# Replacing a per-channel convolution on transposed input by banded matmuls on untransposed input

## The chip, the cores and the metric

The kernel runs on one core of a Trainium2 chip. The metric is the device time of one execution in microseconds (us). A profile comes from one profiled execution; its span is the time between its first and its last instruction, and the execution's own time is a little longer.

## What is computed

Input `x` is 8 sequences of 4096 rows with 192 channels. Stage one is a causal convolution over the rows with 7 taps; the 192 channels are 8 heads of 24 channels, and the 7 weights of a head (a softmax of 7 numbers) are shared by its channels. Stage two is a two-layer map with 2048 hidden units and the activation h·cos(h).

```python
w = softmax(weight)                       # 8 heads x 7 taps
x_pad = concat([zeros(B, 6, D), x])       # 6 rows of zeros ahead of each sequence
out = einsum('hk,bskhg->bshg', w, x_unf)  # x_unf[b, s, k] = x_pad[b, s + k]
h = out @ w_in                            # 32768 x 192 @ 192 x 2048
return (h * cos(h)) @ w_out               # @ 2048 x 192
```

## The kernel before

The 32768 rows are cut into 64 tiles of 512 rows, 8 to a sequence. All matmuls are bf16 and sum in fp32. The body is written as a loop over the tiles, but the order in which instructions stand on each engine is fixed when the program is built: a scheduler mixes the steps of neighbouring tiles on each engine, and each engine then goes through its own list in order, waiting on semaphores where a step needs another engine's result. The buffers come from pools that rotate: `x_bf`, `xT`, `xT_o`, `conv_sb` and `g_sb` two each, `x_f32`, `cos_sb` and `o_sb` three; of the PSUM tiles `h_ps` three, and `ps_t`, `conv_ps` and `o_ps` one each.

For each tile:

- `prep_tile` (L115 to L138): SyncE's queue loads 512 rows into `x_f32` (L118, 384 KB), GpSimd casts them to bf16 in four pieces (`x_bf`, L121), TensorE turns them in 8 transposes (`ps_t`, L126) so that channels lie on the partitions (two halves of 96), and ScalarE copies the two halves out of PSUM (`xT`, L127 and L128). GpSimd puts the last 6 columns of the tile before in front (L133), or zeros at the start of a sequence (L131), and makes a copy of `xT` shifted by one column (`xT_o`, L136), which the odd taps read.
- `conv_tile` (L140 to L152): for each of 7 taps and 2 channel halves one matmul with 512 moving columns (L148), 14 in all, whose weights are a 96x96 diagonal matrix of that tap's weights (`diagW`, L100, made once at the start). They sum in `conv_ps`, and VectorE copies the two halves to `conv_sb` (L150, L151), which is again channels by rows.
- Hidden layer (L161 to L168): for each of 16 blocks of 128 hidden units two matmuls with 512 columns (L164) fill one `h_ps`, ScalarE takes the cosine of it (L167), and VectorE multiplies `h_ps` by the cosine into `g_sb` (L168). An `h_ps` comes free when both have read it.
- Output layer (L174 to L183): for each of 4 pieces of 128 rows 16 matmuls with 192 columns (L180) sum in half of an `o_ps`, and VectorE copies that half out (L182). The second half's matmuls wait for the copy of the first half. The tile's output leaves with one transfer (L183).

In the loop the preparation and convolution of tile it+1 stand between the hidden layer and the output layer of tile it. At the start of the program a chain of small steps on VectorE and ScalarE makes the softmax and `wtab`, from which `diagW` is made, while the two weight matrices are loaded and cast.

## Time and profile before

| what | value |
| --- | --- |
| median of 4 runs | 1119.2 us (1118.15 to 1119.48) |
| the profiled execution's own time | 1119.48 us |
| its span | 1117.7 us |
| TensorE busy (matmuls / weight loads) | 1066.2 us / 684.8 us |
| VectorE, ScalarE, GpSimd busy | 814.4, 699.2, 154.3 us |
| matmuls and weight loads | 7554 of each |
| transfer of a tile's input, issue to landing | 3.4 us |

A row of a group gives the line, the engine, the operation, the tiles that it writes and reads, their shapes, the count, the busy time in us and the mean duration in ns, and then how long the engine was idle just before, and who released it. PEld is the weight load of TensorE, which has records of its own. Matmuls follow each other faster than their durations say, since each includes the way through the array; so the spacing of a run of matmuls is worked out from the run's length less one duration. A row of the timeline gives the start, the length of a run of like instructions, and what they are. The chain of waits is the work that ended last, followed back from the end.

### The profile page before, as it was taken

How to read it: one execution, taken by the hardware profiler on the slowest of the kernel's cores; microseconds unless marked ns; L12 is line 12 of the kernel's file. 1: busy time of each engine (PE TensorE's matmuls, PEld its weight loads, DVE VectorE, ACT ScalarE, POOL GpSimd, SP SyncE). 2: the span in 40 equal slices, each digit the busy share in tenths (PEclk: the TensorE clock that was granted, in tenths of full speed). 3: DMA queues.
4: the chain of work that ended last, by engine and by line, in shares of the span. 5: the costliest groups of instructions: out<-in, count | busy, mean ns of one | idle time of the engine just before them, and what ended most of it. 6: DMA issues, size and time to landing. Idle time of an engine off the chain costs nothing.

```text
span 1117.7 us, 19647 instructions
## 1 busy us (share of the span) xinstructions
PE 1066.2 (95%) x7554; PEld 684.8 (61%) x7554; DVE 814.4 (73%) x1432; ACT 699.2 (63%) x1159; POOL 154.3 (14%) x392
## 2 busy tenths in 40 slices
PE   3999999999999999999999999999999999999997
PEld 2566666566666665666666666666656666666664
DVE  1877777777777777777777777777777777777775
ACT  4765665666656656656656666566566566665663
POOL 2111111111101101111111111011011111111100
PEclk9999999999999999999999999999999999999999
DMA  7111111111101101111111111011011111110000
GB/s 197 44 49 38 57 45 42 57 43 43 57 30 56 58 29 58 54 33 57 45 42 58 43 44 57 29 57 58 29 57 55 32 58 43 43 57 28 16 30 29
DMA packets 69982, 54.74 MB, mean 49 GB/s; under 512 B 2112, under 2 KB 69696, under 8 KB 69696
## 3 DMA queue, kind: packets, MB, share of 16 engines
q1 hardware_dynamic: 69888, 53.49, 15.9%
q8 instruction: 59, 0.97, 0.4%
q14 instruction: 35, 0.29, 0.1%
HBM read 28.31 MB, written 25.17 MB: 48 GB/s over the span
## 4 chain that ended last, share of the span: by engine, by line
PE 66%; ACT 15%; issue 9%; POOL 6%; DMA 1%; DVE 1%; POOLq 0%; SPq 0%; ACTq 0%
PE o_ps L180 25%; PE h_ps L164 22%; PE conv_ps L148 16%; ACT cos_sb L167 10%; POOL xT_o L136 6%; ACT xT L128 3%; PE ps_t L126 2%; ACT xT L127 2%; DMA x_f<-in_x_dram 1%; POOL x_bf L121 1%; DVE g_sb L168 1%; DVE conv_sb L150 0%; DVE o_sb L182 0%; POOLq L209 0%; POOLq L136 0%
## 5 line engine op out<-in xcount | busy, mean ns | idle before, releaser
L167 ACT ACTIVATE cos_sb<-h_ps,halfpi 128x512 bf16<-128x512 f32 x1024 | 644.2, 692 | 391.1 <-PE h_ps L164 390.3
L168 DVE TENSOR_TENSOR g_sb<-h_ps,cos_sb 128x512 bf16<-128x512 f32 x1024 | 654.6, 686 | 222.9 <-ACT cos_sb L167 222.1
L164 PE MATMUL h_ps<-conv_sb,w_in_sb 96*128 96x512 bf16 x2048 | 561.9, 378 | 18.9 <-DVE g_sb L168 12.4
L180 PE MATMUL o_ps<-w_out_sb,g_sb 128*128 128x192 bf16 x4096 | 433.2, 246 | 2.3 <-DVE o_sb L182 1.3
L180 PEld LDWEIGHTS <-g_sb 128*128 128x128 bf16 x4096 | 349.6, 97 | 114.5 <-issue 24.5
L164 PEld LDWEIGHTS <-w_in_sb 96*128 96x128 bf16 x2048 | 195.1, 97 | 181.0 <-issue 39.1
L121 POOL CAST x_bf<-x_f 128x192 bf16<-128x192 f32 x256 | 78.4, 346 | 759.1 <-PE ps_t L126 734.3
L148 PEld LDWEIGHTS <-diagW 96*96 96x96 bf16 x896 | 110.5, 123 | 107.7 <-issue 19.4
L148 PE MATMUL conv_ps<-xT,diagW 96*96 96x512 bf16 x512 | 164.9, 382 | 1.0 <-ACT xT L127 1.0
L148 PE MATMUL conv_ps<-xT_o,diagW 96*96 96x512 bf16 x384 | 116.2, 382 | 9.0 <-POOL xT_o L136 8.4
L182 DVE COPY o_sb<-o_ps 128x192 f32<-128x192 f32 x256 | 89.6, 350 | 10.7 <-PE o_ps L180 5.8
L136 POOL COPY xT_o<-xT 96x1034 bf16<-96x1034 bf16 x64 | 67.2, 1050 | 174.5 <-ACT xT L128 174.5
L150 DVE CAST conv_sb<-conv_ps 96x512 bf16<-96x512 f32 x64 | 43.9, 686 | 55.6 <-PE conv_ps L148 55.6
L126 PE MATMUL ps_t<-ident,x_bf 128*96 128x128 bf16 x512 | 51.2, 222 | 10.7 <-POOL x_bf L121 10.7
L126 PEld LDWEIGHTS <-x_bf 128*96 128x96 bf16 x512 | 40.1, 125 | 19.9 <-POOL x_bf L121 10.8
L151 DVE CAST conv_sb<-conv_ps 96x512 bf16<-96x512 f32 x64 | 43.3, 677 | 0.0
L127 ACT COPY xT<-ps_t 96x512 bf16<-96x512 bf16 x64 | 37.2, 581 | 7.0 <-PE ps_t L126 7.0
L128 ACT COPY xT<-ps_t 96x512 bf16<-96x512 bf16 x64 | 37.8, 591 | 0.0
L133 POOL COPY xT<-xT 96x12 bf16<-96x12 bf16 x56 | 10.7, 191 | 0.0
L100 DVE TENSOR_SCALAR diagW<-ident,wtab 96x96 bf16<-96x96 bf16 x14 | 2.2, 238 | 6.8 <-ACT wtab L79 6.8
L76 PE MATMUL wtab_ps<-wsm,sel 8*96 8x7 bf16 x2 | 0.3, 225 | 5.5 <-DVE sel L73 5.5
L94 ACT CAST w_out_sb<-w_out_f 128x3072 bf16<-128x3072 f32 x1 | 2.8, 2752 | 2.7 <-DMA w_out_f<-in_moe_w_out_dram 2.7
(26 smaller groups left out, 11.2 us busy)
## 6 DMA issues: line engine op xcount, KB each, us to landing
x_f<-in_x_dram SPq DMA_DIRECT2D x64, 384.0 KB, 3.4
out_dram<-o_sb SPq DMA_DIRECT2D x64, 384.0 KB, 2.6
w_in_f<-in_moe_w_in_dram SPq DMA_DIRECT2D x2, 768.0 KB, 7.2
w_out_f<-in_moe_w_out_dram SPq DMA_DIRECT2D x1, 1536.0 KB, 12.8
w_sb<-in_weight_dram SPq DMA_DIRECT2D x1, 0.2 KB
```

The lines of the kernel that those rows point to most:

```text
L121: nc.gpsimd.tensor_copy(out=x_bf[:, s, :], in_=x_f32[:, s, :])
L126: nc.tensor.transpose(ps_t[:, c, s, :], x_bf[:, s, c * HD : (c + 1) * HD], ident)
L127: nc.scalar.copy(xT[:, 0, PAD:], ps_t[:, 0, :, :])
L128: nc.scalar.copy(xT[:, 1, PAD:], ps_t[:, 1, :, :])
L136: nc.gpsimd.tensor_copy(out=xT_o[:, :, 0 : T + PAD - 1], in_=xT[:, :, 1 : T + PAD])
L148: nc.tensor.matmul(out=conv_ps[:, c, :], lhsT=diagW[:, c * K + k, :], rhs=rhs_src, start=(k == 0), stop=(k == K - 1))
L150: nc.vector.tensor_copy(out=conv_sb[:, 0, :], in_=conv_ps[:, 0, :])
L164: nc.tensor.matmul(out=h_ps, lhsT=w_in_sb[:, c, f * 128 : (f + 1) * 128], rhs=conv_sb[:, c, :], start=(c == 0), stop=(c == 1))
L167: nc.scalar.activation(out=cos_sb, in_=h_ps, func=AF.Sin, bias=halfpi, scale=1.0)
L168: nc.vector.tensor_tensor(out=g_sb[:, f, :], in0=h_ps, in1=cos_sb, op=ALU.mult)
L180: nc.tensor.matmul(out=o_ps[:, s2, 0:D], lhsT=g_sb[:, f, s * 128 : (s + 1) * 128], rhs=w_out_sb[:, f, :], start=(f == 0), stop=(f == NF - 1))
L182: nc.vector.tensor_copy(out=o_sb[:, s, :], in_=o_ps[:, s2, 0:D])
```

## The change

The convolution is no longer done on the transposed input with one diagonal matrix per tap. It is done on the input as it was loaded, rows on the partitions: the weights of a matmul are now a 128x128 banded matrix, one for each head (`band`), which holds the 7 taps on 7 diagonals, and the moving operand is the 24 channels of that head. A second matrix (`bandhi`) adds what reaches over from the next 128 rows. So each 128 rows take 8 heads x 2 matmuls with 24 columns, and a tile 64 of them in place of 14 with 512 columns. Their result (`ct_ps`, a PSUM tile for two pieces of 128 rows, two of them) is copied to `ct_sb`, by VectorE for the first piece and by ScalarE for the second. Only then come the 8 transposes, and ScalarE and VectorE copy a half each to `convT`, which the hidden layer reads where it read `conv_sb`.

The input is loaded 6 rows earlier, so that row r of a block holds the first tap of output row r. The last block of a tile needs 6 more rows: they come by a small transfer of their own (`hx`, 6x192) and go through a buffer that GpSimd has set to zero (L157 to L160). At the start of a sequence VectorE clears 6 rows of `x_f32` and the load is split in two. Removed are `xT`, the shifted copy `xT_o` (L136), the copying of the last 6 columns (L133) and `diagW`. The preparation of tile it+2 now follows the convolution of tile it+1; before, the preparation of it+1 stood ahead of it.

At the start of the program 8 copies on ScalarE spread the softmax weights, one matmul hands them to all 128 partitions (`wb`), and VectorE builds `band` with 8 multiplications and 48 multiply-adds of 128x128 and `bandhi` with 11 small products and sums.

```diff
+    for ci in range(K - 1):
+        wv = wb3[:, :, 6 - ci : 7 - ci].to_broadcast([128, H, PAD])
+        mv = mc[:, ci : ci + 1, :].to_broadcast([128, H, PAD])
+        nc.vector.tensor_tensor(out=bh if ci == 0 else htmp, in0=mv, in1=wv, op=ALU.mult)
+        if ci:
+            nc.vector.tensor_tensor(out=bh, in0=bh, in1=htmp, op=ALU.add)
+    for h in range(H):
+        b = band[:, h, :]
+        nc.vector.tensor_scalar(out=b, in0=identx[:, 0:128], scalar1=wb[:, h * K : h * K + 1], scalar2=None, op0=ALU.mult)
+        for k in range(1, K):
+            nc.vector.scalar_tensor_tensor(out=b, in0=identx[:, k : k + 128], scalar=wb[:, h * K + k : h * K + k + 1],
+                                           in1=b, op0=ALU.mult, op1=ALU.add)
...
     def prep_tile(it):
...
-        nc.sync.dma_start(out=x_f32, in_=xf[t0 : t0 + T, :].rearrange("(n p) d -> p n d", p=128))
+        if it % TPB == 0:
+            nc.vector.memset(x_f32[0:PAD, 0, :], 0.0)
+            nc.sync.dma_start(out=x_f32[PAD:128, 0, :], in_=xf[t0 : t0 + 128 - PAD, :])
+            nc.sync.dma_start(out=x_f32[:, 1:4, :],
+                              in_=xf[t0 + 128 - PAD : t0 + T - PAD, :].rearrange("(n p) d -> p n d", p=128))
+        else:
+            nc.sync.dma_start(out=x_f32, in_=xf[t0 - PAD : t0 + T - PAD, :].rearrange("(n p) d -> p n d", p=128))
...
-        xT = xT_pool.tile([HD, 2, T + PAD], BF16)
-        ps_t = xtp.tile([HD, 2, 4, 128], BF16)
-        for c in range(2):
-            for s in range(4):
-                nc.tensor.transpose(ps_t[:, c, s, :], x_bf[:, s, c * HD : (c + 1) * HD], ident)
-        nc.scalar.copy(xT[:, 0, PAD:], ps_t[:, 0, :, :])
-        nc.scalar.copy(xT[:, 1, PAD:], ps_t[:, 1, :, :])
...
-        nc.gpsimd.tensor_copy(out=xT_o[:, :, 0 : T + PAD - 1], in_=xT[:, :, 1 : T + PAD])
+        hx = hx_pool.tile([128, 2, D], FP32)
+        nc.sync.dma_start(out=hx[0 : PAD, 0, :], in_=xf[t0 + T - PAD : t0 + T, :])
+        nc.gpsimd.memset(hx[:, 1, :], 0.0)
+        nc.gpsimd.tensor_copy(out=hx[0:PAD, 1, :], in_=hx[0:PAD, 0, :])
+        hx_bf = hx_pool.tile([128, D], BF16)
+        nc.gpsimd.tensor_copy(out=hx_bf, in_=hx[:, 1, :])
...
     def conv_tile():
-        for k in range(K):
-            for c in range(2):
-                rhs_src = xT[:, c, k : k + T] if k % 2 == 0 else xT_o[:, c, k - 1 : k - 1 + T]
-                nc.tensor.matmul(out=conv_ps[:, c, :], lhsT=diagW[:, c * K + k, :],
-                                 rhs=rhs_src, start=(k == 0), stop=(k == K - 1))
-        nc.vector.tensor_copy(out=conv_sb[:, 0, :], in_=conv_ps[:, 0, :])
-        nc.vector.tensor_copy(out=conv_sb[:, 1, :], in_=conv_ps[:, 1, :])
+        for sp in range(2):
+            ct_ps = ct_ps_pool.tile([128, 2, D], FP32)
+            for s2 in range(2):
+                s = sp * 2 + s2
+                nxt = x_bf[:, s + 1, :] if s < 3 else state["hx_bf"]
+                for h in range(H):
+                    nc.tensor.matmul(out=ct_ps[:, s2, h * G : (h + 1) * G], lhsT=band[:, h, :],
+                                     rhs=x_bf[:, s, h * G : (h + 1) * G], start=True, stop=False)
+                    nc.tensor.matmul(out=ct_ps[:, s2, h * G : (h + 1) * G], lhsT=bandhi[:, h, :],
+                                     rhs=nxt[:, h * G : (h + 1) * G], start=False, stop=True)
+                if s2 == 0:
+                    nc.vector.tensor_copy(out=ct_sb[:, s, :], in_=ct_ps[:, s2, :])
+                else:
+                    nc.scalar.copy(ct_sb[:, s, :], ct_ps[:, s2, :])
         ps_t = xtp.tile([HD, 2, 4, 128], BF16)
         for c in range(2):
             for s in range(4):
-                nc.tensor.transpose(ps_t[:, c, s, :], x_bf[:, s, c * HD : (c + 1) * HD], ident)
+                nc.tensor.transpose(ps_t[:, c, s, :], ct_sb[:, s, c * HD : (c + 1) * HD], ident)
+        nc.scalar.copy(convT[:, 0, :], ps_t[:, 0, :, :])
+        nc.vector.tensor_copy(out=convT[:, 1, :], in_=ps_t[:, 1, :, :])
```

How the order on the engines changes is seen at three places in the middle of the program. The first is TensorE's list in the kernel before, where the convolution of the next tile (`conv_ps`) is reached: `h_ps` belongs to the hidden layer, `o_ps` to the output layer, and the engine named in brackets is the one whose semaphore the row waits for.

```order
L180 MATMUL o_ps<-w_out_sb,g_sb 128x192
L148 LDWEIGHTS diagW
L148 MATMUL conv_ps<-xT_o,diagW 96x512 [waits Pool_49]
L148 LDWEIGHTS diagW
L148 MATMUL conv_ps<-xT_o,diagW 96x512
L164 LDWEIGHTS w_in_sb
L164 MATMUL h_ps<-conv_sb,w_in_sb 128x512 [waits DVE_49]
L164 LDWEIGHTS w_in_sb
L164 MATMUL h_ps<-conv_sb,w_in_sb 128x512
L148 LDWEIGHTS diagW
L148 MATMUL conv_ps<-xT,diagW 96x512
```

The convolution's third and fourth matmul wait there for GpSimd's shifted copy, and all that stands behind them waits with them. In the changed kernel TensorE's list has, at the place where the second 128 rows of a `ct_ps` begin:

```order
L201 MATMUL h_ps<-convT,w_in_sb 128x512 [waits DVE_49]
L201 LDWEIGHTS w_in_sb
L201 MATMUL h_ps<-convT,w_in_sb 128x512
L174 LDWEIGHTS band
L174 MATMUL ct_ps<-x_bf,band 128x24 [waits DVE_49]
L176 LDWEIGHTS bandhi
L176 MATMUL ct_ps<-hx_bf,bandhi 128x24 [waits Pool_49]
L174 LDWEIGHTS band
L174 MATMUL ct_ps<-x_bf,band 128x24
L176 LDWEIGHTS bandhi
L176 MATMUL ct_ps<-hx_bf,bandhi 128x24
```

Each matmul of 24 columns has a weight load of its own ahead of it; the first one waits for VectorE's copy of the first 128 rows out of the same PSUM tile, and the first one that reads `hx_bf` for GpSimd.

The second place is TensorE's list in the changed kernel a little ahead of these rows, where the transposes (`ps_t`) of the finished 128-row pieces stand:

```order
L201 LDWEIGHTS w_in_sb
L201 MATMUL h_ps<-convT,w_in_sb 128x512 [waits DVE_49]
L201 LDWEIGHTS w_in_sb
L201 MATMUL h_ps<-convT,w_in_sb 128x512
L218 LDWEIGHTS g_sb
L218 MATMUL o_ps<-w_out_sb,g_sb 128x192
L185 LDWEIGHTS ct_sb [waits Activation_49]
L185 MATMUL ps_t<-ident,ct_sb 96x128
L201 LDWEIGHTS w_in_sb
L201 MATMUL h_ps<-convT,w_in_sb 128x512 [waits DVE_49]
```

The transposes, which opened the preparation before, now follow the convolution, and matmuls of the output and the hidden layer stand between them.

The third place is ScalarE's list in one tile, before:

```order
L167 ACTIVATE cos_sb<-h_ps,halfpi 128x512 [waits DVE_49,PE_49] x8
L127 COPY xT<-ps_t 96x512 [waits PE_49,Pool_49]
L167 ACTIVATE cos_sb<-h_ps,halfpi 128x512 [waits DVE_49,PE_49] x3
L128 COPY xT<-ps_t 96x512
L167 ACTIVATE cos_sb<-h_ps,halfpi 128x512 [waits DVE_49,PE_49] x4
```

and in the changed kernel:

```order
L204 ACTIVATE cos_sb<-h_ps,halfpi 128x512 [waits DVE_49,PE_49] x13
L181 CAST ct_sb<-ct_ps 128x192 [waits PE_49]
L204 ACTIVATE cos_sb<-h_ps,halfpi 128x512 [waits DVE_49,PE_49] x3
L181 CAST ct_sb<-ct_ps 128x192 [waits DVE_49,PE_49]
L204 ACTIVATE cos_sb<-h_ps,halfpi 128x512 [waits DVE_49,PE_49] x2
L186 COPY convT<-ps_t 96x512 [waits PE_49]
```

Two copies of 512 columns between the cosines have become two of 192 columns and one of 512.

89 lines of the change are left out of this document (49 added, 40 removed).

## The prediction

> **What bounds the kernel now.** I read the page first, for the engines and the chain of waits.
>
> ```profile
> span 1117.7 us, 19647 instructions
> PE 1066.2 (95%) x7554; PEld 684.8 (61%) x7554; DVE 814.4 (73%) x1432; ACT 699.2 (63%) x1159; POOL 154.3 (14%) x392
> PE 66%; ACT 15%; issue 9%; POOL 6%; DMA 1%; DVE 1%; POOLq 0%; SPq 0%; ACTq 0%
> ```
>
> TensorE is busy nearly throughout, but a third of the chain lies elsewhere: ScalarE, GpSimd and "issue". So a matmul saved and a wait saved may both count. Next I read one tile in the timeline, for its period and for the spacing of each kind of matmul.
>
> ```profile
> 504.47 0.37 SPq L183 DMA_DIRECT2D out_dram<-o_sb  x1
> ...
> 511.40 0.59 PE L148 MATMUL conv_ps<-xT_o,diagW 96*96 96x512 bf16 x2
> ...
> 512.70 0.59 PE L148 MATMUL conv_ps<-xT,diagW 96*96 96x512 bf16 x2
> ...
> 513.54 0.55 PE L126 MATMUL ps_t<-ident,x_bf 128*96 128x128 bf16 x7
> ...
> 515.14 1.49 PE L180 MATMUL o_ps<-w_out_sb,g_sb 128*128 128x192 bf16 x16
> ...
> 520.74 1.46 PE L164 MATMUL h_ps<-conv_sb,w_in_sb 96*128 96x512 bf16 x6
> ...
> 521.49 0.37 SPq L183 DMA_DIRECT2D out_dram<-o_sb  x1
> ```
>
> ```profile
> L164 PE MATMUL h_ps<-conv_sb,w_in_sb 96*128 96x512 bf16 x2048 | 561.9, 378 | 18.9 <-DVE g_sb L168 12.4 <-DVE conv_sb L150 1.0
> L180 PE MATMUL o_ps<-w_out_sb,g_sb 128*128 128x192 bf16 x4096 | 433.2, 246 | 2.3 <-DVE o_sb L182 1.3 <-DVE g_sb L168 1.0
> L180 PEld LDWEIGHTS <-g_sb 128*128 128x128 bf16 x4096 | 349.6, 97 | 114.5 <-issue 24.5 <-DVE g_sb L168 2.3
> L126 PE MATMUL ps_t<-ident,x_bf 128*96 128x128 bf16 x512 | 51.2, 222 | 10.7 <-POOL x_bf L121 10.7
> L126 PEld LDWEIGHTS <-x_bf 128*96 128x96 bf16 x512 | 40.1, 125 | 19.9 <-POOL x_bf L121 10.8 <-issue 0.9
> ```
>
> A tile's output leaves every 521.49 - 504.47 = 17.02 us, and 64 tiles make 1089 us of the span. Spacing is a run less one duration, over the steps between: hidden layer (1.46 - 0.378)/5 = 0.2164 us, output layer (1.49 - 0.246)/15 = 0.0829, transposes (0.55 - 0.222)/6 = 0.055. The two convolution rows are six matmuls apart: 1.30/6 = 0.217. Each spacing is shorter than the matmul's own duration, and the transposes' 0.055 is even shorter than their weight load's 0.125: loads run under the matmuls ahead of them. A tile then needs on TensorE 32 x 0.2164 + 64 x 0.0829 + 14 x 0.217 + 8 x 0.055 = 6.92 + 5.31 + 3.04 + 0.44 = 15.71 us, and 17.02 - 15.71 = 1.31 us are waits. The chain in order of time, and the engines' busy time in that stretch, say where.
>
> ```profile
> 506.08 0.39 ACT xT L127
> ...
> 508.28 0.60 ACT xT L128
> ...
> 509.00 1.06 POOL xT_o L136
> ...
> 510.11 0.59 PE conv_ps L148 x2
> ```
>
> ```profile
> 504.33:510.11 5.78, 5.33 (x31) 2.79 (x30) 4.50 (x9) 5.75 (x11) 2.33 (x6) 1.00 0.46 136
> ```
>
> From 504.33 to 510.11 ScalarE is the last (5.75 of 5.78 us busy: nine cosines and the two copies), then GpSimd's shifted copy; TensorE drips one hidden block at a time. From 510.11 on TensorE alone sets the pace. This is the wait that the change addresses.
>
> **Part by part.** *Convolution on TensorE.* Out go 3.04 us a tile. In come 64 pairs of a 128x128 weight load and a matmul of 24 columns; the trace has no such pair, and all hangs on its spacing p. From below: 24 columns at the output layer's rate, 24/192 x 0.0829 = 0.010 us. From above, hidden: the transposes, 128 columns and a load each, go at 0.055, so a pair with fewer columns and the quicker load (97 ns against 125) should not need more. From above, not hidden: the whole 0.097 of a load. The nearest in size are two matmuls of 7 columns at the start.
>
> ```profile
> 5.46 0.31 PE L76 MATMUL wtab_ps<-wsm,sel 8*96 8x7 bf16 x2 [5.46 <-DVE sel L73]
> ...
> 22.87 1.06 PE L148 MATMUL conv_ps<-xT,diagW 96*96 96x512 bf16 x2
> ...
> 23.73 1.06 PE L148 MATMUL conv_ps<-xT_o,diagW 96*96 96x512 bf16 x2
> ...
> L76 PE MATMUL wtab_ps<-wsm,sel 8*96 8x7 bf16 x2 | 0.3, 225 | 5.5 <-DVE sel L73 5.5
> ```
>
> They are 0.31 - 0.225 = 0.085 apart, at a time when the clock is low: the convolution's matmuls there are (23.73 - 22.87)/2 = 0.43 apart, twice the 0.217 of later. Halved, 0.085 is 0.0425, with a 96-column load; I take p = 0.040, so 64 x 0.040 = 2.56 us a tile. Transposes, hidden and output layer stay: 6.92 + 5.31 + 0.44 = 12.67. Sum 15.23, 0.48 less.
>
> *The waits.* The hop over GpSimd (1.06 us) is gone: the banded matmuls read `x_bf`, which GpSimd casts a whole tile early.
>
> ```profile
> L167 ACT ACTIVATE cos_sb<-h_ps,halfpi 128x512 bf16<-128x512 f32 x1024 | 644.2, 692 | 391.1 <-PE h_ps L164 390.3
> L121 POOL CAST x_bf<-x_f 128x192 bf16<-128x192 f32 x256 | 78.4, 346 | 759.1 <-PE ps_t L126 734.3 <-DMA x_f<-in_x_dram 14.4 <-issue 10.4
> L136 POOL COPY xT_o<-xT 96x1034 bf16<-96x1034 bf16 x64 | 67.2, 1050 | 174.5 <-ACT xT L128 174.5
> L127 ACT COPY xT<-ps_t 96x512 bf16<-96x512 bf16 x64 | 37.2, 581 | 7.0 <-PE ps_t L126 7.0
> L150 DVE CAST conv_sb<-conv_ps 96x512 bf16<-96x512 f32 x64 | 43.9, 686 | 55.6 <-PE conv_ps L148 55.6
> L182 DVE COPY o_sb<-o_ps 128x192 f32<-128x192 f32 x256 | 89.6, 350 | 10.7 <-PE o_ps L180 5.8
> 1109.77 0.36 DVE L182 COPY o_sb<-o_ps 128x192 f32<-128x192 f32 x1 [1.57 <-PE o_ps L180]
> 1110.19 1.48 PE L180 MATMUL o_ps<-w_out_sb,g_sb 128*128 128x192 bf16 x16 [0.45 <-DVE o_sb L182]
> x_f<-in_x_dram SPq DMA_DIRECT2D x64, 384.0 KB, 3.4
> ```
>
> What is late next is ScalarE again: 16 cosines of 644.2/1024 = 0.63 us, while only three `h_ps` exist. Its copies cost about the same as before (2 x 0.35 + 0.58 = 1.28 us against 2 x 0.58 = 1.16, a 192-column copy priced by VectorE's), VectorE's too (2 x 0.35 + 0.69 against 2 x 0.69). But TensorE has some fifty pairs that need neither, and the order puts them among the hidden blocks. Bounds of the remaining wait: 0 if they fill everything, 1.31 if nothing is gained; I take the half, 0.65. New waits: the second 128 rows of each `ct_ps` wait for VectorE's copy of the first, the transposes for ScalarE's copy, and everything behind on TensorE waits with them. Uncovered, one costs 0.42 us, as at the end of the program (1109.77 to 1110.19), where nothing stands between. In the order, hidden and output matmuls stand between, so I count them at nothing; that cover gone is a rival. On ScalarE and VectorE the copies that wait hold the cosines and products behind them; they wait for pairs that TensorE has done before it turns to other blocks, so again nothing.
>
> *GpSimd and SyncE.* GpSimd loses 1.05 us a tile and gains a zeroing, a small copy and a cast, by the 0.346 us of its cast at most 1.0 together; it was busy 14%. SyncE gets one 4.6 KB transfer per tile more and, eight times, the input in two; the input is issued over a tile ahead of its use and lands in 3.4 us. If the small transfer waited for its buffer, the output and the next input behind it on SyncE's queue would wait as well; with a tile of slack I count nothing.
>
> *The start.*
>
> ```profile
> 5.06 0.34 DVE L73 TENSOR_TENSOR sel<-ge,le 8x192 bf16<-8x192 f32 x1
> ...
> 12.20 2.25 DVE L100 TENSOR_SCALAR diagW<-ident,wtab 96x96 bf16<-96x96 bf16 x14 [6.79 <-ACT wtab L79]
> ...
> 18.76 1.07 PE L148 MATMUL conv_ps<-xT,diagW 96*96 96x512 bf16 x2 [0.67 <-ACT xT L127]
> ...
> 26.23 1.46 PE L164 MATMUL h_ps<-conv_sb,w_in_sb 96*128 96x512 bf16 x6 [0.67 <-DVE conv_sb L150]
> ```
>
> Before, convolution starts at 18.76 us, after the input has landed, and the first hidden block at 26.23. Now VectorE has 56 steps of 128 columns and some 11 small ones after about 7 us. By the spacing of the 14 multiplications (2.25/14 = 0.16) they end near 18 us, hidden by the input; by the 0.34 of the product at 5.06 they end near 30. At 0.25, 56 x 0.25 + 11 x 0.2 = 16.2, they end at 23.2; the last pairs, two copies, the transposes and two copies more make 4 to 7 us, so the first hidden block stands near 30, 4 later. Bounds 0 and 10.
>
> *Sum.* Per tile 15.23 + 0.65 = 15.88, 1.14 less than 17.02; 64 x 1.14 = 73 us less, 4 more at the start. The profiled execution took 1119.48 us, 0.3 more than the median of 1119.2: 1119.5 - 73 + 4 = 1050 us.
>
> **The rivals.** *A: the weight loads show.* If a load is not hidden by a matmul of 24 columns, each pair takes the 0.097 of its row: 6.21 us a tile, 18.88 with the rest, with 0.3 of waits 19.18; 64 x 2.16 + 4 = 142 more, 1262 us. It decides from p = (17.02 - 0.06 - 0.45 - 12.67)/64 = 0.060 on. Against it: both the output layer and the transposes hide theirs, the latter at 0.055. For it: they have more columns to hide under. The Trainium skill (TensorE: Matmul & The Clock Gate, Back-to-back issue gap) gives about 81 ns per matmul for a stream of load and matmul pairs at 128 columns; the transposes' 0.055 does not agree, and by its figure the change would be estimated as slower, near 1196 us.
>
> *B: pairs are cheaper.* Midway between 0.010 and 0.0425, p = 0.026: 1.66 us a tile, less work to fill the waits, say 1.0: 15.33, 64 x 1.69 - 4 = 104 less, 1015 us. For it: the 7-column pairs had loads of 96 columns, the slower kind (125 against 97 ns). The same section of the Trainium skill has an issue floor of about 25 ns for matmuls of up to 64 columns; no row here shows it yet.
>
> *C: pairs cost as much as transposes,* 0.055: 3.52, with 0.45 of waits 16.64; 64 x 0.38 - 4 = 20 less, 1099 us. For it: each pair is two instructions, and no pair in the trace goes faster at the high clock.
>
> *D: the copies show.* If the two waits for VectorE's copy, the wait for ScalarE's last copy and the two halves of `convT` (0.6 each) stood open in every tile, that is 3 x 0.42 + 1.2 = 2.5 us: 15.23 + 2.5 = 17.7, 64 x 0.7 + 4 = 49 more, 1168 us. It decides from 17.02 - 0.06 - 15.23 = 1.73 us on. Against it: the work that stands between in the order.
>
> **How the numbers follow.** Forecast (p from 0.033 to 0.047) 0.40, B 0.28, C 0.19, A 0.08, D 0.05. B's lower end, p = 0.022 with 1.1 of waits, is 15.18 a tile, 64 x 1.84 - 4 = 114 less, 1006; C with the start 10 late in place of 4 and 0.05 more of waits is 1099 + 6 + 3 = 1108. From 1005 to 1108 the range holds the forecast and most of B and C. A difference of 0.2%, about 2 us, is what a measurement can tell here. Faster: the forecast, B, and C but for 0.02: 0.85; within 0.2%: 0.02; slower: A and D, 0.13.
>
> **What would show it.** Right: a run of ct_ps pairs at 0.033 to 0.047 each, outputs leaving every 15.6 to 16.1 us, GpSimd gone from the chain, the first hidden block near 30 us. Pairs at 0.06 or more mean A; TensorE idle before ct_ps or ps_t behind a VectorE or ScalarE copy, by more than 1.7 us a tile, means D; a hidden layer that waits for ScalarE as long as before means that the half I took off the waits is wrong.

## The result and the profile after

| | before | changed |
| --- | --- | --- |
| median | 1119.21 us (1118.15 to 1120.04, 13 runs) | 992.46 us (991.91 to 992.95, 8 runs) |
| ratio | | 0.8868, 95% interval 0.886 to 0.8877 |
| span of the profiled execution | 1117.7 us | 990.6 us |

The medians and ratios here and below leave out two slow executions, one of e3_before_no_hop (1799.22 us at a granted clock of 0.561) and one of e9_rows64 (1563.5 us at 0.816).

The change takes off 127 us, almost twice the 69 that were forecast, and the time lies below the range. The page of the changed kernel, its engines and its chain of waits by engine and by line:

```profile
span 990.6 us, 26393 instructions
PE 959.8 (97%) x10753; PEld 681.2 (69%) x10753; DVE 811.7 (82%) x1567; ACT 720.7 (73%) x1230; POOL 140.2 (14%) x459
PE 96%; DMA 1%; ACT 1%; DVE 1%; POOL 0%; issue 0%; SPq 0%; POOLq 0%
```

TensorE was 66% of the chain and is now 96%; GpSimd's 6% is gone, and ScalarE's 15% is 1%. So the time is nearly the sum of TensorE's work, and the price of a pair decides. The timeline shows it, in the middle of the run:

```profile
507.05 0.81 PE L201 MATMUL h_ps<-convT,w_in_sb 96*128 96x512 bf16 x3
507.82 1.48 PE L218 MATMUL o_ps<-w_out_sb,g_sb 128*128 128x192 bf16 x16
...
510.22 0.18 PE L174 MATMUL ct_ps<-x_bf,band 128*128 128x24 bf16 x1
510.25 0.17 PE L176 MATMUL ct_ps<-x_bf,bandhi 128*128 128x24 bf16 x1
...
510.65 0.17 PE L176 MATMUL ct_ps<-x_bf,bandhi 128*128 128x24 bf16 x1
```

From 510.22 to 510.65 stand 18 matmuls of pairs (the middle ones are left out here), 0.43/17 = 25 ns apart, though every one has its own load of 128x128 weights, which takes 96 ns by its records on the page. The forecast had 40 ns for the spacing. Hidden and output matmuls keep their spacing. The outputs leave at these times, the third and the fifty-ninth:

```profile
78.94 0.41 SPq L221 DMA_DIRECT2D out_dram<-o_sb  x1
...
913.40 73.91 SPq L221 DMA_DIRECT2D out_dram<-o_sb  x6
```

The outputs' own rows give the first and the last, of the changed kernel and of the one before:

```profile
L221 SPq DMA_DIRECT2D out_dram<-o_sb x64: 372/384/406, 50.5 to 986.9; - x64
```

```profile
L183 SPq DMA_DIRECT2D out_dram<-o_sb x64: 372/372/388, 48.9 to 1114.0; - x64
```

The steady period is (913.40 - 78.94)/56 = 14.90 us, where it was 17.02. TensorE needs 6.92 + 5.31 + 0.44 + 64 x 0.025 = 14.27 of it, and 0.63 are waits. From first to last output it is 936.4 us in place of 1065.1, which is 128.7 less; the first output is 1.6 later. That loss goes with TensorE's pace at the start: two hidden matmuls take 0.59 us at 30 us in the kernel before, and still 1.06 in the changed one, where 0.59 is reached only after 34 us. The rows of the changed kernel and of the one before:

```profile
30.89 1.06 PE L201 MATMUL h_ps<-convT,w_in_sb 96*128 96x512 bf16 x2
```

```profile
29.91 0.59 PE L164 MATMUL h_ps<-conv_sb,w_in_sb 96*128 96x512 bf16 x2
```

What TensorE still waits for, by the table of waits (us in total, times, longest):

```profile
PEld L185 <- ACT ct_sb L181: 23.0, 83, 0.5
PEld L218 <- issue: 18.1, 75, 0.6
PEld L218 <- DVE g_sb L205: 7.8, 25, 0.8
```

PEld is TensorE's weight load. The largest is a new wait, the transposes' for ScalarE's copy of `ct_sb`: 23.0/64 = 0.36 us a tile. The second 128 rows' wait for VectorE's copy is 0.4 us in the whole run.

### The profile page after: what moved, and what is told of

It reads as the page before. It is cut to its first block, busy times and chain, and to the rows that moved or that the text cites. A ratio compares the mean times of both kernels' runs of the same rounds, so it can differ in the third digit from the quotient of the medians.

```text
span 990.6 us, 26393 instructions
## 1 busy us (share of the span) xinstructions
PE 959.8 (97%) x10753; PEld 681.2 (69%) x10753; DVE 811.7 (82%) x1567; ACT 720.7 (73%) x1230; POOL 140.2 (14%) x459
## 4 chain that ended last, share of the span: by engine, by line
PE 96%; DMA 1%; ACT 1%; DVE 1%; POOL 0%; issue 0%; SPq 0%; POOLq 0%
PE h_ps L201 46%; PE o_ps L218 35%; PE ct_ps L176 5%; PE ct_ps L174 5%; PE ps_t L185 4%; DMA x_f<-in_x_dram 1%; ACT convT L186 1%; POOL x_bf L154 0%; ACT cos_sb L204 0%; DVE g_sb L205 0%; DVE o_sb L220 0%; SPq L119 0%; SPq L125 0%; SPq L49 0%; DVE ct_sb L179 0%
## 5 line engine op out<-in xcount | busy, mean ns | idle before, releaser
L201 PE MATMUL h_ps<-convT,w_in_sb 96*128 96x512 bf16 x2048 | 579.1, 380 | 2.4 <-DVE g_sb L205 0.4
L174 PE MATMUL ct_ps<-x_bf,band 128*128 128x24 bf16 x2048 | 148.8, 174 | 15.9 <-DVE band L112 12.3
L174 PEld LDWEIGHTS <-band 128*128 128x128 bf16 x2048 | 131.6, 96 | 45.7 <-DVE band L114 9.5
L176 PEld LDWEIGHTS <-bandhi 128*128 128x128 bf16 x2048 | 125.9, 96 | 45.4 <-issue 13.4
L176 PE MATMUL ct_ps<-x_bf,bandhi 128*128 128x24 bf16 x1536 | 116.0, 173 | 0.2
L185 PEld LDWEIGHTS <-ct_sb 128*96 128x96 bf16 x512 | 53.8, 123 | 42.5 <-ACT ct_sb L181 23.0
L185 PE MATMUL ps_t<-ident,ct_sb 128*96 128x128 bf16 x512 | 81.1, 231 | 0.1
L179 DVE CAST ct_sb<-ct_ps 128x192 bf16<-128x192 f32 x128 | 43.5, 349 | 5.2 <-PE ct_ps L176 5.2
L181 ACT CAST ct_sb<-ct_ps 128x192 bf16<-128x192 f32 x128 | 40.6, 319 | 5.3 <-PE ct_ps L176 5.2
L186 ACT COPY convT<-ps_t 96x512 bf16<-96x512 bf16 x64 | 36.5, 570 | 1.0 <-PE ps_t L185 1.0
L160 POOL CAST hx_bf<-hx 128x192 bf16<-128x192 f32 x64 | 22.0, 344 | 0.1
L157 POOL MEMSET hx<- 128x192 f32 x64 | 16.4, 258 | 3.7
```

Of the source, the lines that this page charges most:

```text
L174: nc.tensor.matmul(out=ct_ps[:, s2, h * G : (h + 1) * G], lhsT=band[:, h, :], rhs=x_bf[:, s, h * G : (h + 1) * G], start=True, stop=False)
L176: nc.tensor.matmul(out=ct_ps[:, s2, h * G : (h + 1) * G], lhsT=bandhi[:, h, :], rhs=nxt[:, h * G : (h + 1) * G], start=False, stop=True)
L179: nc.vector.tensor_copy(out=ct_sb[:, s, :], in_=ct_ps[:, s2, :])
L181: nc.scalar.copy(ct_sb[:, s, :], ct_ps[:, s2, :])
L185: nc.tensor.transpose(ps_t[:, c, s, :], ct_sb[:, s, c * HD : (c + 1) * HD], ident)
L186: nc.scalar.copy(convT[:, 0, :], ps_t[:, 0, :, :])
```

## The experiments

My theory after the two traces: a pair costs 25 ns whatever its columns, which is the whole of the missed gain, and the waits are as forecast. Rivals: the pair costs its load or its columns, and 25 ns is chance; or the gain came from waits. A second question is what made the row wrong from which the prediction took p. All times below are medians; the ratio is to the kernel before, timed on the same chip, with its 95% interval.

| run | time, us | ratio |
| --- | --- | --- |
| e1_halves, 128 pairs of 12 columns | 1082.49 | 0.9682 (0.9665 to 0.9698) |
| e2_wide48, 32 pairs of 48 | 980.55 | 0.8767 (0.8754 to 0.8781) |
| e2b_wide96, 16 pairs of 96 | 964.32 | 0.8623 (0.861 to 0.8636) |
| e6_k6, second matmul on 6 rows | 1570.53 | 1.4045 (1.4024 to 1.4066) |
| e9_rows64, on 64 rows | 1548.84 | 1.3838 (1.3782 to 1.3894) |
| e9b_rows32, on 32 rows | 1548.2 | 1.3849 (1.383 to 1.3868) |
| e12_wtab16 (before, 16 small pairs) | 1119.58 | one execution |
| e14_forms (changed, forms at its end) | 992.8 | one execution |
| e3_before_no_hop, no shifted copy | 1086.56 | 0.9702 (0.9685 to 0.9718) |
| e5_hps4, four `h_ps` | 1053.5 | 0.9406 (0.939 to 0.9422) |
| e7_rowmajor, transposes' loops exchanged | 990.12 | 0.8844 (0.883 to 0.8857) |
| e8_half_bands, half the bands built | 989.44 | 0.8835 (0.8823 to 0.8848) |
| e11_gpsimd_bands, two bands by GpSimd | 991.9 | 0.887 (0.8858 to 0.8882) |
| e13_strided96, 16 pairs, same result | 963.72 | 0.8616 (0.8603 to 0.8629) |
| e15_strided48, 32 pairs, same result | 965.68 | 0.8629 (0.8615 to 0.8644) |
| e16_scalar_copies, e13 with ScalarE's copies | 973.8 | 0.8703 (0.8691 to 0.8715) |

### What a pair costs

**e1_halves: twice as many pairs, half as wide.**

```diff
-                for h in range(H):
-                    nc.tensor.matmul(out=ct_ps[:, s2, h * G : (h + 1) * G], lhsT=band[:, h, :],
-                                     rhs=x_bf[:, s, h * G : (h + 1) * G], start=True, stop=False)
+                for q in range(2 * H):
+                    h, G2 = q // 2, G // 2
+                    nc.tensor.matmul(out=ct_ps[:, s2, q * G2 : (q + 1) * G2], lhsT=band[:, h, :],
+                                     rhs=x_bf[:, s, q * G2 : (q + 1) * G2], start=True, stop=False)
...
```

> Each banded matmul of 24 columns is split into two of 12 with the same weights, so a tile has 128 pairs in place of 64 and computes the same. Theory 1 (a pair costs a fixed 25 ns however few its columns are, with its weight load hidden): the spacing stays at 25 ns, a tile needs 64 x 0.025 = 1.6 us more on TensorE, of which at most the 0.63 us of waits that remain can be filled: 992 + 64 x (1.0 to 1.6) = 1056 to 1095 us. Rival (the 25 ns belong to 24 columns and shrink with them): spacing near 13 ns, 985 to 1000 us.

The timeline, with 30 steps from the first row to the last:

```profile
507.01 0.17 PE L175 MATMUL ct_ps<-x_bf,band 128*128 128x12 bf16 x1
...
507.76 0.17 PE L175 MATMUL ct_ps<-x_bf,band 128*128 128x12 bf16 x1
```

The spacing stays 25 ns, and the time rises by 90 us: 64 more pairs of 25 ns are 1.6 us a tile, 102 us over 64, of which some 0.2 us a tile went into waits that were there. Fewer columns save nothing at this size; each pair costs 25 ns.

**e2_wide48 and e2b_wide96: fewer, wider pairs.** A matmul takes two or four heads' columns with the first head's weights; the other heads' weights are left out. The second matmul is edited alike; with 96 columns the step is 4.

```diff
-                for h in range(H):
-                    nc.tensor.matmul(out=ct_ps[:, s2, h * G : (h + 1) * G], lhsT=band[:, h, :],
-                                     rhs=x_bf[:, s, h * G : (h + 1) * G], start=True, stop=False)
+                for h in range(0, H, 2):
+                    nc.tensor.matmul(out=ct_ps[:, s2, h * G : (h + 2) * G], lhsT=band[:, h, :],
+                                     rhs=x_bf[:, s, h * G : (h + 2) * G], start=True, stop=False)
...
```

> Two heads share one pair of 48 columns, with the weights of the first of the two: 32 pairs a tile, the other head's taps are left out. Theory 1 (fixed 25 ns): spacing 25 ns again, since 48 columns at the output layer's rate (0.0829/192 each) are 21 ns; 0.8 us a tile less, 992 - 51 = 941, to 955 if waits take some of it back. Rival (the cost grows with the columns, or a fixed part plus a column part): spacing 36 to 50 ns, 32 x 0.036 to 0.05 = 1.15 to 1.6 us, 963 to 995 us.

> Four heads share one pair of 96 columns, with the weights of the first of the four: 16 pairs a tile, the other heads' taps are left out. Theory 1 (the larger of 25 ns and the columns' own time): 96 columns at the output layer's rate are 41 ns, so the spacing is 41 to 44 ns, 16 x 0.042 = 0.67 us a tile, 0.93 less: 992 - 59 = 933, to 950 if the waits grow. If a floor were a property of the weight load alone and added to the columns, the spacing would be 25 + 41 = 66 ns, 1.06 us a tile and 958 us or more.

The timeline of the first and of the second:

```profile
507.68 0.18 PE L174 MATMUL ct_ps<-x_bf,band 128*128 128x48 bf16 x1
507.70 0.18 PE L176 MATMUL ct_ps<-x_bf,bandhi 128*128 128x48 bf16 x1
```

```profile
513.34 0.20 PE L174 MATMUL ct_ps<-x_bf,band 128*128 128x96 bf16 x1
513.38 0.20 PE L176 MATMUL ct_ps<-x_bf,bandhi 128*128 128x96 bf16 x1
```

48 columns still go at 25 ns, 96 at 41: the spacing is the larger of 25 ns and the columns' own time (0.43 ns each, as at 192 and 512), and the load lies under it. Both times lie above what theory 1 put and where the rivals had them; it is the spacing that decides for theory 1. Of the 51 us that 32 fewer pairs save, the 48-column run shows only 12, and the 96-column one 28 of some 60. Much of the rest became waits; the table of the first:

```profile
PEld L185 <- ACT ct_sb L181: 51.1, 113, 0.6
PEld L218 <- DVE g_sb L205: 25.0, 64, 0.7
```

The transposes' wait has grown by 28 us and the one for VectorE's products from 7.8 to 25: TensorE is no longer the only bound.

**e6_k6, e9_rows64, e9b_rows32: fewer rows in the second matmul.** Only 6 rows of `bandhi` are not zero. In e6_k6 the second matmul and its load take these 6, and GpSimd's zeroing goes; in the others 64 and 32.

```diff
-                    nc.tensor.matmul(out=ct_ps[:, s2, h * G : (h + 1) * G], lhsT=bandhi[:, h, :],
-                                     rhs=nxt[:, h * G : (h + 1) * G], start=False, stop=True)
+                    nc.tensor.matmul(out=ct_ps[:, s2, h * G : (h + 1) * G], lhsT=bandhi[0:PAD, h, :],
+                                     rhs=nxt[0:PAD, h * G : (h + 1) * G], start=False, stop=True)
...
```

> The second matmul of each pair, for what reaches over from the next 128 rows, uses only the 6 rows of its weights and of its operand that are not zero; the buffer that GpSimd zeroed is then not needed, and GpSimd's zeroing and one of its two small steps are gone. It computes the same. Theory 1 (fixed 25 ns, a load's size hidden; GpSimd far from the bound): same within 0.5%, 988 to 997 us, and spacing still 25 ns. Rival (the rows that a load or a matmul reads set the price): half of the pairs get cheaper, up to 32 x 0.02 = 0.64 us a tile, 951 to 975 us.

It missed by over 570 us, which is why the other two were run:

> The changed kernel, where the second matmul of each pair (and its weight load) takes 64 rows in place of 128; only rows 0 to 5 of its weights are not zero, so the result is the same. With 6 rows the pairs' matmuls went 114 to 119 ns apart and the run took 1570 us. Theory 1 (any change of the row count between neighbours costs it): 110 to 120 ns per matmul again and about 1400 to 1580 us. Rival 1 (it is the small count, in which few of the array's rows are used, that costs it; hidden blocks with 96 rows and output blocks with 128 follow each other in the changed kernel at no cost): 25 ns and 985 to 1000 us.

> As the last one, with 32 rows in place of 64. Theory 1 (any change of the row count): 110 to 120 ns per matmul and about 1400 to 1580 us. Rival 1 (small counts alone): 25 ns and 985 to 1000 us if 32 rows are enough, 110 to 120 ns if they still are too few; with the run of 64 rows this brackets the point.

The timeline with 64 rows, and two windows of the same run (the last three columns: granted clock, share of the DMA engines, GB/s):

```profile
503.12 0.18 PE L176 MATMUL ct_ps<-x_bf,bandhi 64*128 64x24 bf16 x1
...
503.83 0.18 PE L176 MATMUL ct_ps<-x_bf,bandhi 64*128 64x24 bf16 x1
```

```profile
500.00:515.00 15.00, 15.00 (x125) 10.54 (x123) 9.60 (x18) 8.44 (x14) 1.22 (x5) 0.98 0.17 54
516.00:530.00 14.00, 14.00 (x84) 8.66 (x82) 5.12 (x10) 5.06 (x9) 2.08 (x7) 0.50 0.10 30
```

Six steps take 0.71 us, so each step between 128 and 64 rows costs 0.12 us, as with 6 and 32 rows: 64 x (0.117 - 0.025) = 5.9 us a tile, 377 over the run. The other 180 to 200 go with stretches at half the clock (0.50 in the second window); the mean granted clock is 0.835, 0.823 and 0.809 with 64, 32 and 6 rows, where the changed kernel has 1.000. What makes the clock fall is open. Theory 1's numbers hold in both runs, but as worded it goes too far: hidden blocks with 96 rows and output blocks with 128 follow each other at no such price in all these kernels.

**e12_wtab16 and e14_forms: which property of a pair costs.** The first repeats the two small pairs at the start of the kernel before, from which the prediction took its p; the second puts nine runs of 16 matmuls of 24 columns behind the changed kernel's last tile.

```diff
-    for c in range(2):
+    for c in [0, 1] * 8:
         nc.tensor.matmul(out=wtab_ps[:, c * K : (c + 1) * K], lhsT=sel[:, c * HD : (c + 1) * HD], rhs=wsm,
                          start=True, stop=True)
```

> The kernel before, with the two matmuls of 7 columns at its start (8 rows, 96 columns of weights) issued eight times over, 16 in a row with a weight load each; the result is the same. The prediction took its p from the 85 ns between the two, halved for the low clock. Theory 1 (the first step after an idle time is longer, and two matmuls show only that): the first two stand about 85 ns apart or more, all later ones 25 to 30, low clock or not. Rival (85 ns is the steady spacing of such pairs at the low clock): all about 85. A third outcome would be above 85 throughout, if matmuls with few rows are slow even when all have the same count.

```diff
+    def one(r, m):
+        return dict(out=ct_ps[0:m, 0, 0:24], lhsT=ident[0:r, 0:m], rhs=mv[0:r, :], start=True, stop=True)
+    for _ in range(16):
+        nc.tensor.matmul(**one(128, 128))
...
```

> The changed kernel, and behind its last tile nine runs of 16 matmuls of 24 columns, each with its own weight load, whose results nobody reads: 128, 96, 64 and 8 rows with 128 columns of weights; 128 and 8 rows with 96 columns of weights; and 128x128 in turn with 96x128, 64x128 and 128x96. It asks what made the pair before the prediction 85 ns, and what made the 6-, 32- and 64-row pairs 114 to 119. Theory 1 (a load goes ahead under the running matmul only if it takes more than 64 rows, or the matmul does): 25 ns for 128 and 96 rows and for 128 in turn with 96; 75 to 120 ns for 64 and 8 rows, alone or in turn; 96 columns of weights alone cost nothing (25 to 45 ns). Rival 1 (only a change of the row count costs): 64 and 8 rows alone at 25 ns, in turn at 115. Rival 2 (weights of 96 columns are what made the old pair slow): 128x96 at 75 ns or more, 8x128 at 25.

The first run's timeline, and the second's:

```profile
5.48 1.44 PE L76 MATMUL wtab_ps<-wsm,sel 8*96 8x7 bf16 x16 [5.48 <-DVE sel L73]
```

```profile
979.59 0.55 PE L230 MATMUL ct_ps<-g_sb,ident 128*128 128x24 bf16 x16
979.99 0.35 PE L232 MATMUL ct_ps<-g_sb,ident 96*128 96x24 bf16 x8
...
981.80 0.56 PE L234 MATMUL ct_ps<-g_sb,ident 64*128 64x24 bf16 x16
...
983.72 0.56 PE L236 MATMUL ct_ps<-g_sb,ident 8*128 8x24 bf16 x16
984.21 0.53 PE L238 MATMUL ct_ps<-g_sb,ident 128*96 128x24 bf16 x8
...
986.32 0.88 PE L240 MATMUL ct_ps<-g_sb,ident 8*96 8x24 bf16 x16
...
987.55 0.17 PE L245 MATMUL ct_ps<-g_sb,ident 128*128 128x24 bf16 x1
987.66 0.18 PE L246 MATMUL ct_ps<-g_sb,ident 64*128 64x24 bf16 x1
...
989.30 0.18 PE L246 MATMUL ct_ps<-g_sb,ident 64*128 64x24 bf16 x1
```

A run less one duration (0.17 to 0.19 us), over its steps: 128, 96, 64 and 8 rows all go at 25 to 26 ns as long as the count stays the same, and 128 and 96 in turn too; 128 and 64 in turn at (989.30 - 987.55)/15 = 0.117 us. Weights of 96 columns go at 0.34/7 = 49 ns with 128 rows and 0.69/15 = 46 with 8; weights of 128 and 96 columns in turn at 35 on average. So two separate prices: a step between 128 rows and 64 or fewer, and weights of 96 columns. At the start, 16 in a row stand (1.44 - 0.225)/15 = 81 ns apart: the 85 of the prediction was a steady spacing, as the rival had it, not a first step. Of the forms theory 1 falls; rival 1 holds for the rows, and rival 2 for the columns in part (49, not 75). The Trainium skill (TensorE: Matmul & The Clock Gate, Weight-path perf modes) says that the fast weight load is taken only with 128 columns of weights; 25 against 46 to 49 ns agrees. The Trainium skill also says (TensorEngine Tiling (Array Packing), Key Properties) that a change of the tiling mode drains TensorE, and lists 64 rows as a mode of their own (Available Configurations there); 117 in turn and 25 alone agree, though no run shows the mode itself.

### What the waits are worth

**e3_before_no_hop: the kernel before without GpSimd's shifted copy.**

```diff
-        nc.gpsimd.tensor_copy(out=xT_o[:, :, 0 : T + PAD - 1], in_=xT[:, :, 1 : T + PAD])
...
-                rhs_src = xT[:, c, k : k + T] if k % 2 == 0 else xT_o[:, c, k - 1 : k - 1 + T]
+                rhs_src = xT[:, c, k : k + T]
```

> The kernel before, with one edit: the odd taps read xT itself at an odd column, so GpSimd's shifted copy xT_o (1.06 us between ScalarE's second copy and the first convolution matmul) is gone; the 14 matmuls of 512 columns stay. It prices the hop alone. Theory 1 (the hop was half of the 1.31 us of waits that a tile had): 0.5 to 1.0 us a tile less, 32 to 64 us, 1055 to 1087 us, with the spacing of the convolution's matmuls at 0.217 for odd taps too. Rival 1 (hidden blocks fill that stretch anyway, and the waits are ScalarE's): 1105 to 1120 us. Rival 2 (an odd start column makes a matmul slower, as a misaligned read): the six odd matmuls of a tile at 0.3 us or more, and 1140 us or more.

```profile
512.26 1.90 PE L143 MATMUL conv_ps<-xT,diagW 96*96 96x512 bf16 x8
```

Odd and even taps go at (1.90 - 0.38)/7 = 0.217 us, so rival 2 is out. The hop was worth 32.5 us, 0.51 a tile. With the 64 x (3.04 - 1.60) = 92 us that TensorE saves on the convolution this makes 124.6, against 126.8 measured: the two parts of the change add up to within 2 us.

**e5_hps4 and e7_rowmajor: what the last 0.63 us are.** For the fourth `h_ps`, `wb_ps` comes from a pool that is closed once `wb` is copied.

```diff
-    h_ps_pool = ctx.enter_context(tc.tile_pool(name="h_ps", bufs=3, space=bass.MemoryType.PSUM))
+    h_ps_pool = ctx.enter_context(tc.tile_pool(name="h_ps", bufs=4, space=bass.MemoryType.PSUM))
...
```

> The changed kernel with four buffers of h_ps in place of three (the PSUM space comes from the weight broadcast at the start, whose buffer is given back early). It asks what the 0.63 us a tile are in which TensorE still waits. Theory 1 (they are waits for the convolution's own copies, 23.0 us of it the transposes' for ScalarE's copy of ct_sb): a fourth buffer changes little, 985 to 993 us, and that wait stays near 23 us. Rival (ScalarE's cosines hold the h_ps buffers, so TensorE runs out of hidden blocks to put between): 0.3 to 0.6 us a tile less, 954 to 975 us.

```diff
-        for c in range(2):
-            for s in range(4):
+        for s in range(4):
+            for c in range(2):
                 nc.tensor.transpose(ps_t[:, c, s, :], ct_sb[:, s, c * HD : (c + 1) * HD], ident)
```

> The changed kernel with the loops of the eight transposes exchanged: 128 rows outside, channel half inside. Six of the eight then need only the first three copies of ct_sb, where before already the fourth needed the last, ScalarE's. Theory 1 (this is a new wait on TensorE, 23.0 us in 83 pieces): most of it goes, 968 to 982 us. Rival (the transposes stand spread between other work, and the seventh waits as long as the fourth did; and the first half of convT is ready later): 988 to 997 us.

With the fourth buffer it is 61 us slower, which neither theory had. Its chain of waits, and its table:

```profile
DVE 47%; PE 45%; ACT 4%; DMA 1%; issue 1%; POOL 0%; SPq 0%; POOLq 0%
```

```profile
PEld L218 <- DVE g_sb L205: 63.4, 129, 0.5
```

The scheduler writes another order (eight hidden matmuls in a row ahead of the pairs at 505 us, where the changed kernel has five at 509), and the output matmuls wait for VectorE's products twice a tile, 63.4 us in place of 7.8. The edit also opens the transposes' PSUM pool at a later place; which of the two changed the order is not shown, and what four buffers would bring in the old order is open.

The exchanged loops left the transposes' wait as it was (23.1 us, 62 times). The time is 2.3 us less, within what the rival had; the two intervals just miss each other. The row of the outputs says where it comes from:

```profile
L221 SPq DMA_DIRECT2D out_dram<-o_sb x64: 372/383/406, 47.5 to 984.6; - x64
```

From first to last output it is 937.1 us, against 936.4; the first output leaves 3.0 earlier, and two hidden matmuls take 0.59 us there already at 29.40. So nothing was gained in the loop; the difference lies at the start.

### The start

**e8_half_bands and e11_gpsimd_bands.** The first leaves out the bands of heads 4 to 7; the second has GpSimd build those of heads 6 and 7 (on top of the exchanged loops).

```diff
-    for h in range(H):
+    for h in range(H // 2):
         b = band[:, h, :]
...
-                    nc.tensor.matmul(out=ct_ps[:, s2, h * G : (h + 1) * G], lhsT=band[:, h, :],
+                    nc.tensor.matmul(out=ct_ps[:, s2, h * G : (h + 1) * G], lhsT=band[:, h % 4, :],
```

> The changed kernel, with the bands of heads 4 to 7 left out: those heads use the bands of heads 0 to 3, so half of VectorE's multiply-adds at the start (some 7 us) are gone and VectorE is done near 14.5 us, before the input lands at 17.2. Per tile nothing changes. It asks why GpSimd's first four casts took 1.19 us each and the later ones 0.30. Theory 1 (they were slow because VectorE ran its multiply-adds at the same time): the four casts take 1.2 to 1.6 us together, the first hidden block starts at 22.5 to 23.6 us in place of 26.27, and the time is 2.5 to 4 us less, 988.5 to 990. Rival (they were slow for another reason, as the first of their kind or beside the weights' transfers and ScalarE's copy): the four take over 4 us again, the first hidden block stays near 26, and the time is 991.5 to 993.5.

```diff
+        if h >= 6:
...
+            for k in range(1, K):
+                nc.gpsimd.tensor_scalar(out=btmp, in0=identx[:, k : k + 128], scalar1=wb[:, h * K + k : h * K + k + 1],
+                                        scalar2=None, op0=ALU.mult)
+                nc.gpsimd.tensor_tensor(out=b, in0=b, in1=btmp, op=ALU.add)
+            continue
```

> The changed kernel with the transposes' loops exchanged, and the bands of heads 6 and 7 built by GpSimd (26 multiplications and additions of 128 columns, since it is idle from 3 to 17 us) in place of VectorE. A candidate for a better start. If an operation takes GpSimd about 0.35 us there (as its casts do with VectorE idle), it is done near 15 us, VectorE near 18, and the first hidden block starts 2 to 3 us earlier than at 26.27: 986.5 to 988.5 us. If VectorE's multiply-adds slow GpSimd as they slowed its casts (1.19 us in place of 0.30), its 26 operations end after 25 us and the first hidden block is 2 to 10 us later: 992 to 1000 us.

The timeline of GpSimd, VectorE and TensorE at the start of the changed kernel, then of the one with half the bands, then GpSimd's in the last:

```profile
17.23 4.76 POOL L154 CAST x_bf<-x_f 128x192 bf16<-128x192 f32 x4 [14.13 <-DMA x_f<-in_x_dram]
...
18.26 3.23 DVE L114 SCALAR_TENSOR_TENSOR band<-identx,wb,band 128x128 bf16<-128x128 bf16 x12
...
21.75 0.18 PE L174 MATMUL ct_ps<-x_bf,band 128*128 128x24 bf16 x1 [3.17 <-POOL x_bf L154]
22.95 1.22 POOL L154 CAST x_bf<-x_f 128x192 bf16<-128x192 f32 x4
...
25.47 0.18 PE L176 MATMUL ct_ps<-x_bf,bandhi 128*128 128x24 bf16 x1
...
26.00 0.18 PE L176 MATMUL ct_ps<-x_bf,bandhi 128*128 128x24 bf16 x1
...
26.27 1.44 PE L201 MATMUL h_ps<-convT,w_in_sb 96*128 96x512 bf16 x3
```

```profile
17.93 0.94 POOL L154 CAST x_bf<-x_f 128x192 bf16<-128x192 f32 x3 [0.35 <-DMA x_f<-in_x_dram]
...
22.93 1.44 PE L201 MATMUL h_ps<-convT,w_in_sb 96*128 96x512 bf16 x3
```

```profile
14.46 0.71 POOL L116 TENSOR_SCALAR btmp<-identx,wb 128x128 bf16<-128x128 bf16 x1
15.25 0.43 POOL L118 TENSOR_TENSOR band<-band,btmp 128x128 bf16<-128x128 bf16 x1
```

Beside VectorE's multiply-adds four casts take 4.76 us; with VectorE done they take 1.2 to 1.3, the first hidden block starts 3.3 us earlier, and the time falls by 3.0. That GpSimd is slow because VectorE runs is thus shown. So giving GpSimd part of the bands gains nothing: its steps take 0.71 and 0.43, the first hidden block starts at 28.37, 2.1 us later than in the changed kernel, and 991.9 us is no better than the 990.1 of e7_rowmajor; that is just under the 992 to 1000 that were put for this case. The Trainium skill (SBUF — State Buffer, Who interferes with whom) names this: a VectorE instruction with two SBUF inputs contends with a GpSimd one that reads SBUF; the casts' 1.19 us beside the multiply-adds, against 0.30 without, agree.

### A faster version

**e13_strided96 and e15_strided48: the same result with 16 or 32 pairs.** One matmul takes a head's columns of four row blocks, or of two.

```diff
+        x_bf = xbf_pool.tile([128, 5, D], BF16)
...
+        for c in range(2):
+            ct_ps = ct_ps_pool.tile([128, 4, HD], FP32)
+            for hh in range(H // 2):
+                h = c * (H // 2) + hh
+                nc.tensor.matmul(out=ct_ps[:, :, hh * G : (hh + 1) * G], lhsT=band[:, h, :],
+                                 rhs=x_bf[:, 0:4, h * G : (h + 1) * G], start=True, stop=False)
+                nc.tensor.matmul(out=ct_ps[:, :, hh * G : (hh + 1) * G], lhsT=bandhi[:, h, :],
+                                 rhs=x_bf[:, 1:5, h * G : (h + 1) * G], start=False, stop=True)
```

> The same result as the changed kernel with a quarter of the pairs: one matmul takes a head's 24 columns of all four row blocks (4 x 24 = 96 columns, a step of 192 between the blocks), hx_bf becomes the fifth block of x_bf, and a ct_ps tile holds the four blocks of four heads. Theory 1 (spacing is the larger of about 25 ns and 0.43 ns a column, steps in the operands cost nothing): 16 pairs at 41 to 43 ns, 0.67 us a tile in place of 1.60, and as in the run with 96 columns much of it becomes waits: 958 to 972 us. Rival 1 (operands in pieces of 24 columns are slower): spacing of 60 ns or more and 972 to 985 us. Rival 2 (both halves' copies must now end before the transposes, which stand bare): spacing as in theory 1 but 980 us or more.

> As the last one with two row blocks in a matmul: 32 pairs of 48 columns, the same result, copies as in the changed kernel. By the run with 48 columns, which left the other heads' weights out, 25 ns and 976 to 986 us. Rival (steps in the operands cost): over 30 ns and 985 us or more.

The timeline with 96 columns:

```profile
501.25 0.20 PE L170 MATMUL ct_ps<-x_bf,band 128*128 128x96 bf16 x1
501.29 0.20 PE L172 MATMUL ct_ps<-x_bf,bandhi 128*128 128x96 bf16 x1
```

Spacing is 41 to 42 ns, and 25 ns with 48 columns: steps in the operands cost nothing. 963.7 us is 29 less than the changed kernel. The 48-column one, at 965.7, is faster than its forecast, and 15 us faster than e2_wide48 with as many pairs: its two copies of a `ct_ps` now both stand behind all of its matmuls, and the transposes' wait for ScalarE has gone (0.4 us in the run, where e2_wide48 has 51.1). The chain of waits with 96 columns shows what is left, and its table of waits:

```profile
PE 72%; DVE 19%; ACT 5%; DMA 2%; issue 1%; POOL 1%; SPq 0%; POOLq 0%
```

```profile
PEld L212 <- DVE g_sb L199: 44.7, 71, 0.7
```

**e16_scalar_copies: less work for VectorE.**

```diff
-            nc.vector.tensor_copy(out=ct_sb[:, 0:2, c * HD : (c + 1) * HD], in_=ct_ps[:, 0:2, :])
-            nc.scalar.copy(ct_sb[:, 2:4, c * HD : (c + 1) * HD], ct_ps[:, 2:4, :])
+            nc.scalar.copy(ct_sb[:, :, c * HD : (c + 1) * HD], ct_ps)
```

> The kernel with 16 pairs of 96 columns (963.7 us), with both copies of a ct_ps half on ScalarE as one of 384 columns, since VectorE is now on the chain of waits with 19% and is the busier of the two (83% against 74%). VectorE loses 2 x 0.347 = 0.69 us a tile; ScalarE has two copies of about 0.5 in place of two of 0.32, 0.36 more. Theory 1 (the waits left are for VectorE's g_sb products, 44.7 + 11.7 us in the table of waits): 948 to 960 us. Rival (they are for the chain from hidden block through cosine to product, so that what ScalarE gains in work comes back): 961 to 975 us.

Its chain of waits:

```profile
PE 66%; ACT 20%; DVE 7%; issue 6%; POOL 1%; DMA 0%; ACTq 0%; POOLq 0%
```

It is 10 us slower. The wait for products falls to 29.6 us, but ScalarE is now 20% of the chain of waits, where it had 5%: its copies stand between the cosines. The time is the rival's: what is left is the chain from hidden block through cosine to product, not VectorE's load alone. That the longer copies on ScalarE are the cause is read from the chain and was not tested apart.

## Why the prediction was wrong

**The step that failed** is "Halved, 0.085 is 0.0425, with a 96-column load; I take p = 0.040". The pair costs 0.025, and 64 x 0.015 = 0.96 us a tile. With 0.025 in its place the forecast's own sum gives 1119.5 - 64 x 2.10 + 4 = 989 us, against 992.4 of the profiled execution. (That it comes so near is in part luck: 64 x 2.10 = 134 us stand against 128.7 from first to last output.) The halving itself was nearly sound: such a pair takes 81 ns at the start and 46 later. (The profile's clock column prints 1.00 at the start as well; that TensorE is slow there rests on the spacing of the matmuls alone.) What was wrong was to carry it over to other weights. With loads of 96 columns a matmul of few columns takes 46 to 49 ns; `band` has 128 columns, and its pairs take 25. The rows count is no rival for this: 8 rows and 128 columns also go at 25. The prediction had the two loads' rows (125 against 97 ns) and gave them to rival B as a reason; in the forecast it priced their difference at 0.0025.

**Rival B** had the mechanism. Its 0.026 was the middle between two bounds, so that it nearly met the number is luck. It put the remaining waits at 1.0, on the ground that less work fills them; they are 0.63, and so it came to 1015. Its page's floor of about 25 ns (the Trainium skill, TensorE: Matmul & The Clock Gate, Back-to-back issue gap) is what the trace shows, at 12, 24 and 48 columns, and with a fresh load for each. The 81 ns that the same section of the Trainium skill gives for pairs with 128 columns is not what this case shows: the transposes go at 55.

**The waits** were right: 0.65 forecast, 0.63 found, and the hop alone is worth 0.51 of the 0.66 by which the forecast cut them. GpSimd is gone from the chain, as forecast. Rival D's copies show with 0.36 us a tile at the transposes, far below the 1.73 from which it decides; that hidden and output matmuls stand between holds. **The start** was put 4 us later and is not: the first hidden block starts at 26.27, 0.04 after that of before. What is lost there, 1.6 us by the first output, goes with TensorE's slow pace up to 34 us, which the prediction did not count. The multiply-adds were priced about right (0.27 us each, 0.25 taken) and end at 21.5 in place of 23.2; what follows takes the lower end of the 4 to 7 us. The slow casts, which the prediction did not see, end just with the bands. **Rivals A and C** fall with the 25 ns.

## What to carry to other kernels

The price of a small matmul is taken from a row whose weight load has the same number of columns, not from the row that is nearest in the matmul's own columns; when a bound from below (0.010) and a row (0.0425) lie a factor of four apart, the whole of a 64-fold term lies between them. A matmul of 12, 24 or 48 columns cost the same 25 ns (the columns' 0.43 ns each take over near 58, worked out from 25/0.43), so columns that share weights are gathered into one matmul with steps in its operands. Once TensorE's sum has fallen that far, count on a quarter to a half of a further saving: of 51 us saved 12 were left in one order of the copies, 27 in another.

## What the runs showed of the hardware

- With 24 columns, a matmul with a fresh 128x128 load takes 25 ns, one with a fresh load of 96 columns 46 to 49.
- A step between matmuls with 128 rows and with 64 or fewer takes 117 to 118 ns in place of 25; 128 and 96 rows alternate freely, and a constant count of 128, 96, 64 or 8 costs nothing. Kernels that alternate on every pair also lose the clock (0.81 to 0.84 on average); why is open.
- The 25 ns hardly change where TensorE is slow: at 26 us, where three hidden matmuls take 1.44 us (0.81 later), the 21 pairs just ahead stand (26.00 - 25.47)/20 = 26.5 ns apart.
- GpSimd's casts take four times as long beside VectorE's multiply-adds (1.19 against 0.30 us).
- Moving operands and results in pieces of 24 columns cost nothing: 96 columns in four pieces go at 41 to 42 ns, as in one piece.
